# Another written-out order for a fused recurrent-attention and maxout kernel: the first weight group ahead of the inputs, and seventeen waits of GpSimd for VectorE

## The chip, the cores and the metric

One Trainium2 chip; the kernel runs on 1 core of it. The metric is device time in microseconds (us): the median of repeated runs of one program. TensorE (PE, with its weight loads PEld) multiplies, VectorE (DVE), ScalarE (ACT) and GpSimd (POOL) do the elementwise work, and SyncE (SP) issues all the transfers here.

## The reference

Two stages follow each other. The first is a gated linear recurrence over 768 steps for 4 batches of 8 heads of width 48; the second is a feed-forward with a maximum of three products, over 3072 tokens of width 384.

```python
state = alpha[:, :, t, :, None] * state + np.einsum('bhd,bhe->bhde', k[:, :, t], v[:, :, t])
y[:, :, t] = np.einsum('bhd,bhde->bhe', q[:, :, t], state)
...
h = np.maximum(np.maximum(x @ w1, x @ w2), x @ w3)
return (h @ w_out).astype(np.float32)
```

## The kernel before, in words

**Tiles and steps.** A step s of 12 covers 256 tokens of one batch (batch s % 4, chunk s // 4). Inputs of a step sit in rings of four buffers, so step s+4 reuses what step s read. Inside a step the recurrence is done in chunks: decays become factors, keys and queries are multiplied by them, scores are masked, and a state of 48 x 48 per head is carried from chunk to chunk. Everything that TensorE writes goes to one of eight banks, which the order names.

**The maxout.** The three products are not computed apart. The weights are staged in three column groups; `differ` forms w2 - w1 and w3 - w1 of a group (wdif), so the hidden value is w1's product plus the larger of zero and the two differences. w1's part is folded into the output: w1 is copied to half precision, turned on TensorE (`turn_weight`), and multiplied with w_out once (`multiply_weights`).

**What sets the order.** The schedule is manual: each engine executes its instructions in the order in which the program issues them, and that order is the string ORDER (line 580), which `emit` walks. A piece reads `letter, number, engine @ step # banks`. Its engine is v (VectorE), p (GpSimd), a (ScalarE); the pieces without one run on TensorE, or on SyncE if they are transfers. The letters, with the line of the operation in the profile where the prediction speaks of it:

- transfers by SyncE: l0 to l3 load alpha, k, q, v of a step (L81); K0 to K11 load weights (L97, L100), three for each column group (w1, w2, w3), then w_out; D turns a half of a step's q and k by a transposing DMA (L310); W stores (L520)
- gates of the recurrence: m pair product of alpha (L225), N logs (L229), r logs and their exponential (L234, L236), c running sums on TensorE (L251, L254), e and f the factors for k and q (L260), g totals (L270), M gates between chunks (L397)
- keys, queries, values: u and w multiply k and q by the nearer alpha (L239, L242), k and q scale them (L280), V scales v (L188 on ScalarE, L190 on VectorE), v copies values for each chunk (L182, L184)
- T turns q and k on TensorE in steps 0 to 4 (L303), and t copies them out (L182, L184); S state products (L408), s adds the kept state (L420), z decays it (L424), y spreads it
- A scores (L324), a masks them (L335, L339), Y attention into x (L350), x copies x out (L182, L184)
- weights: b copy to half precision, B turn (L449), n keep, d differences (L438), C w_out in half precision, P product (L460)
- G gates of the maxout (L472), h the two maxima (L481, L483, L485), O projections (L506), o scaled output (L188, L190)
- I spreads the mask over rows, Z clears padding, H issues warming matmuls on a blank tile (L525), `H..^name` the same after one small matmul that waits for a named tile (L544).

A group's first three weights are staged in ring buffers of steps 2 and 3 (`staged`): K0 in alpha's third buffer, K1 in q's, K2 in k's. So a load for step 2 waits until the copy and the differences of that group have read them.

A piece with `>name` gets an explicit wait of its first instruction for the named piece's last one; everything else waits only for the data and buffers that it uses.

The lists start in this order of loads: alpha0, alpha1, k0, q0, k1, K1, v0, K0, K2, q1, v1, alpha4. In the list before, twelve pieces carry a `>`.

Of the kernel before, what the change touches and what calls it, by code (L numbers as in the profile page):

```python
# [24 lines left out]
def kernel(  # L25
# [552 lines left out]
    held = mybir.DependencyInfo(mybir.DependencyClass.Sync, mybir.DependencyReason.DATA)  # L578

    ORDER = """  # L580
        l0@0 l0@1 l1@0 l2@0 Z2a@0 m0v@0 l1@1 N0a@0 r0a@0 H10@0#0 c0@0#0 K1@0 e0a@0 m0p@1 I0a@0 l3@0 u0v@0 N0a@1
        K0@0 k0v@0 r1a@0 H7@0#1 c0@1#1 K2@0 f0a@0 w0v@0 e0a@1 l2@1 r0a@1 q0v@0 l3@1 r1a@1 g0a@1 u0v@1 g0a@0
        H6@0#2 T1@0#2 l0@4 T0@0#3 k0p@1>u0@1 t1v@0 t0v@0 V0a@0 H1@0#4 H1^t1@0#4 A1@0#4,5 M0p@1 M0p@0 S0@0#6,7
        d0v@0 s0a@0 f0a@1 z0v@0 b0a@0 a2v@0 K3@0 y0a@0 d1v@0 H2@0#0 H2^d0@0#0 B0@0#0 A0@0#2,3 w0v@1 Y3@0#6 l0@2
        K4@0 q0v@1 K5@0 V0a@1 a1v@0 l2@2 H4@0#1 T0@1#1 a0v@0 T1@1#4 v1p@1>q0@1 t0a@1 a3v@0 S0@1#3,2 l1@2 Z3v@0
        t1a@1 Y0@0#5 s0v@1 m0v@4 r0a@4 v0v@1 K6@0 A0@1#1,4 r1a@4 n0v@0 x0a@0 z0v@1 H1@0#3 A1@1#3,0 a0v@1 x1a@0
        m0p@2>z0@1 y0a@1 a1v@1 H1@0#1 G0@0#1 d2v@0 N0a@2 h0a@0 c0@2#5 b1v@0 r0a@2 K7@0 G2@0#6 d3v@0 N0a@4 K8@0
        r1a@2 a3v@1 e0a@2 l3@2 H1@0#4 G3@0#4 w0p@2>d3@0 h2a@0 a2v@1 c0@4#1 f0a@2 l0@3 Y3@1#6 s1v@1 Y0@1#0 q0v@2
        Y2@1 x0a@1 G1@0#3 K9@0 g0a@4 x1a@1 h3v@0 u0p@2>q0@2 B1@0#2 e0a@4 G2@1#0 h1v@0 n1a@0 k0v@2 G0@1#6 h2a@1
        G3@1#4 g0a@2 f0a@4 d4v@0 h0a@1 T0@2#2 b2a@0 T1@2#3 K10@0 t0v@2 d5p@0>d4@0 G1@1#0 l1@4 t1a@2 s1v@0 h3v@1  # L590
        G4@1#5 K11@0 V0a@2 h1v@1 A0@2#1,6 A1@2#2,3 M0p@2 M1p@0 a0v@2 l0@5 S0@2#7,4 v0p@2 a2v@2 G5@0#0 s0a@2
        v1a@2 l2@4 a1v@2 G5@1#7 z0p@2 a3v@2 m0p@3 G4@0#1 y0a@2 s1v@2 Y0@2#2 z1p@0 N0a@3 Y2@2#6 x0v@2 Y3@2 B2@0#3
        y1p@0 l1@3 x1a@2 c0@3#4 h4a@0 n2v@0 G2@2#2 g0a@3 h4a@1 G1@2#3 u0p@4 h2a@2 h5v@1 G0@2#6 r0a@3 e0a@3 k0v@4
        G5@2#1 C1a@0 G3@2#5 l2@3 M0v@3 C0v@0 C2a@0 G4@2#7 h5v@0 P1@0#2 l3@4 h4v@2 m0p@5>C0@0 h3v@2 P0@0#0 M0p@4
        p1a@0 l3@3 w0v@4 r0a@5 P2@0#7 N0a@5 q0v@4 p0a@0 r1a@3 c0@5#2 p2v@0 T1@4#5 f0a@3 l0@6 e0a@5 u0v@3 T0@4#0
        h5v@2 O0@0#4 t0a@4 l0@7 k0v@3 h0a@2 w0v@3 O1@0#7 f0a@5 l1@5 h1v@2 V0a@4 q0p@3>w0@3 t1v@4 g0a@5 O0@1#1
        l0@8 V0a@3 o1v@0 o0v@0 v1p@4 r1a@5 r0a@6 W0@0 S0@4#0,6 S0@3#3,5 o0a@1 s0v@4 A0@4#2,7 M1p@1 s0v@3 v1a@3
        W1@0 T0@3#4 z0p@4 l2@5 T1@3#0 z0p@3 s1v@4 l1@6 O0@2#1 a1v@4 m0p@6 t1a@3 l3@6 t0v@3 y0p@4 v0a@4 a0v@4
        A1@3#3,6 A1@4#7,0 s1v@3 m0p@7 A0@3#4,2 a2v@3 r1a@6 O1@1#5 N0a@6 a2v@4 m0p@8 o0a@2 a0v@3 v0a@3 l2@6 u0p@5
        c0@6#3 a3v@3 O1@2#7 a1v@3 N0a@7 z1p@1 l0@9 y0a@3 a3v@4 k0p@5 Y1@4#4 Y3@4#1 l3@5 Y0@3#6 Y3@3#2 Y2@3 x0v@3  # L600
        Y0@4 x1a@3 Y2@4 o1v@1 u0p@6 c0@7#0 e0a@6 G1@3#6 o1v@2 x1a@4 N0a@8 w0v@5 G2@3#2 f0a@7 q0v@5 G4@3#1 f0a@6
        e0a@7 c0@8#5 h2v@3 x0a@4 D0@5 G3@3#7 g0a@6 h4a@3 V0v@6 G5@3#2 r0a@7 h3v@3 v1p@6>V0@6 D1@5 e0a@8 G0@3#4
        h5v@3 f0a@8 G4@4#7 m0v@9 h0a@3 k0v@6 G0@4#3 N0a@9 r0a@8 G3@4#1 l1@7 w0v@6 g0a@7 g0a@8 W0@2 V0a@5 G2@4#2
        h1v@3 q0p@6>w0@6 h4v@4 c0@9#4 h0a@4 G5@4#6 l2@7 h2v@4 g0a@9 G1@4#7 h5v@4 M0p@6 f0a@9 D0@6 M1p@4 O1@3#0
        v1p@5 h1v@4 e0a@9 v0a@5 h3v@4 D1@6 M0p@5 M1v@5 M1v@2 u0v@7 A1@5#5,2 v0a@6 A0@5#3,6 S0@5#7,4 O0@3#1 s0v@5
        r0a@9 a2v@5 z0p@5 y1a@1 W0@1 a0v@5 M1p@3 l3@7 z1p@2 O1@4#7 s1v@5 y0p@5 y1a@2 a1v@5 l1@8 a3v@5 k0p@7
        r1a@7 l3@8 r1a@8 Y3@5#5 o1v@4 Y2@5 Y0@5#3 x1a@5 Y1@5 o0v@3 S0@6#4,6 x0a@5 A1@6#2,7 w0p@7 a3v@6 o1a@3
        G4@5#1 W1@1 M0p@7 a2v@6 G5@5#5 q0p@7 s0v@6 G2@5#3 h4v@5 V0a@7 A0@6#0,7 h5v@5 G0@5#2 z0p@6 h2a@5 D1@7
        a0v@6 z1p@4 v0a@7 G1@5#4 a1v@6 z1p@3 G3@5#1 D0@7 h0v@5 y0a@6 y1p@3 O0@4#5 s1v@6 h1v@5 v1p@7 h3v@5 l2@8
        Y3@6#3 o0a@4 z1v@5 Y2@6 l1@9 M0v@8 Y1@6#0 u0v@8 Y0@6 V0a@8 O1@5#7 k0v@8 W0@3 r1a@9 x0a@6 x1v@6 y1a@5  # L610
        S0@7#2,6 l0@10 S0@8#4 s0v@7 y1a@4 A0@7#5,1 W1@2 A1@7#0,3 z0p@7 a1v@7 G0@6#2 l0@11 y0a@7 w0p@8 s0v@8
        G2@6#1 a3v@7 v1a@8 G5@6#4 a2v@7 q0p@8 h2v@6 G4@6#3 h0a@6 a0v@7 G3@6#0 h4a@6 Y3@7#1 z0p@8 h5v@6 D0@8 Y2@7
        Y1@7#2 M0p@9 Y0@7 u0p@9 h3v@6 G1@6#5 r0a@10 x1v@7 l2@9 O0@5#3 m0p@10 s1v@7 D1@8 x0v@7 h1v@6 G0@7#4 o1v@5
        m0v@11 G4@7#0 l1@10 h0a@7 k0v@9 G5@7#1 N0a@11 c0@11#6 l3@9 G2@7#2 e0a@11 N0a@10 G3@7#4 h2v@7 g0a@11
        f0a@11 l3@10 G1@7#5 M1p@7 h4v@7 w0p@9 v0a@8 c0@10#7 h3v@7 O1@6#2 g0a@10 h5v@7 q0p@9 y0a@8 h1v@7 e0a@10
        A0@8#0,4 r1a@10 A1@8#6,1 a0v@8 O0@7#5 M1p@6 D0@9 z1p@6 a2v@8 V0a@9 M0p@10 a1v@8 u0p@10 D1@9 O0@6#0 a3v@8
        V0a@10 o0v@5 f0a@10 k0v@10 Y2@8#6 W0@4 y1a@6 Y0@8#4 W1@4 Y3@8 Y1@8 z1v@7 S0@9#7 x1v@8 x0a@8 S0@10#1
        v0a@10 s0v@9 O1@7#3 l2@10 z0v@9 W1@3 s0v@10 l3@11 z0p@10 l1@11 o1a@6 v0p@9>z0@9 A0@9#4,6 A1@9#7,1 r0a@11
        a1v@9 G0@8#2 y0a@9 a3v@9 v1p@9 G1@8#6 h0a@8 a0v@9 l2@11 G4@8#1 a2v@9 G3@8#4 o0a@6 w0v@10 Y2@9#2 Y1@9#7
        o0a@7 h1v@8 Y0@9 q0p@10>w0@10 Y3@9 G2@8#0 x1a@9 x0a@9 G5@8#6 h4a@8 h2v@8 G0@9#5 r1a@11 D0@10 h5v@8  # L620
        V0a@11 u0p@11 G2@9#2 h3v@8 h0a@9 G5@9#0 D1@10 w0v@11 v0a@11 G1@9#7 k0v@11 G3@9#1 h2a@9 W0@5 q0v@11
        G4@9#6 M0v@11 O0@8#4 h1v@9 D1@11 h4a@9 h3v@9 y0a@10 h5v@9 D0@11 v1a@11 S0@11#5 A0@10#2,6 A1@10#7,1
        O1@9#0 a3v@10 o1a@7 W1@5 W1@6 a0v@10 s0v@11 O1@8#1 W1@7 a2v@10 z0p@11 W0@7 a1v@10 W0@6 v1p@10 A0@11#2,3
        A1@11#5,7 y0p@11 a1v@11 O0@9#6 a0v@11 y1p@7 a2v@11 Y1@10#3 a3v@11 Y0@10 Y2@10#2 x0a@10 Y3@10 Y1@11#5
        Y0@11 x1a@10 Y2@11#7 x0v@11 Y3@11 G1@10#3 x1a@11 o1v@8 o1a@9 G4@10#5 W1@9 G3@11#2 W1@8 h4a@10 G2@10#7
        o0a@9 G2@11#0 G5@10#5 h2v@11 G0@10#6 h3v@11 G0@11#1 h0a@10 h2v@10 G3@10#0 h5v@10 G5@11#2 h3v@10 G4@11#7
        h1v@10 G1@11#6 h0v@11 h4a@11 O0@10#5 h1v@11 h5v@11 O2@11#0 o0a@10 o0a@8 O1@10#7 W0@8 W0@9 W0@10 O3@11
        O4@11#3,5 o0a@11 o1v@10 W1@10 W0@11 O6@11 O5@11 o2a@11 o1v@11 W2@11 W1@11
# [42 lines left out]
```

## Time and profile before

| | |
|---|---|
| runs | 140.74 us median of 3 (139.72 to 141.44) |
| profiled execution | 140.59 us, of which the span is 138.9 |
| granted TensorE clock | 0.996 |
| DMA | 32.32 MB, mean 233 GB/s |

The profile numbers times from the start of the span. A row of the timeline gives start, duration, engine, line, operation, output and inputs with shapes, a count where neighbours are merged, and in brackets how long the engine was idle before it and what ended that. A row of the chain gives start, duration and what it was. Matmuls are pipelined, so the duration of a merged row has a tail that overlaps with the next. A row by stage gives the stage's bounds and length, then busy time of each engine with its count of instructions, the granted clock, the DMA share and GB/s. A row of waits gives who waited for what, in total, how often, and the longest.

### The profile page before, as it was taken

The page shows a single profiled execution, that of the slowest core. Times are in us where ns is not written, and L with a number is a line of the kernel's source. Part 1 is how long each engine was busy: PE and PEld are TensorE (multiplying, and loading weights), DVE is VectorE, ACT ScalarE, POOL GpSimd, SP SyncE. Part 2 cuts the span into 40 slices and gives each one's busy share as a digit, 9 for nine tenths or more (in the row PEclk, how much of TensorE's full clock was granted, in tenths as well). Part 3 has the DMA queues.
Part 4 walks back from the last instruction along what each step waited for, and adds up shares of the span by engine and source line. Part 5 has one row for each costly group of instructions (what it writes and reads, how often), then busy time and mean ns, then how long its engine had stood idle before and what let it go on. Part 6 is the DMA issues. An engine that isn't in the chain of part 4 may idle for free.

```text
span 138.9 us, 5317 instructions
## 1 busy us (share of the span) xinstructions
PE 129.5 (93%) x2231; PEld 94.9 (68%) x2231; DVE 112.2 (81%) x211; ACT 100.1 (72%) x217; POOL 63.2 (45%) x103
## 2 busy tenths in 40 slices
...
GB/s 102 325 341 351 336 326 276 315 288 295 327 238 242 237 322 292 298 186 91 285 155 330 204 293 327 124 187 310 127 246 330 186 168 275 110 111 7 0 170 170
DMA packets 72743, 32.32 MB, mean 233 GB/s; under 512 B 65296, under 2 KB 72720, under 8 KB 72720
## 3 DMA queue, kind: packets, MB, share of 16 engines
...
## 4 chain that ended last, share of the span: by engine, by line
PE 64%; ACT 11%; DVE 10%; issue 4%; POOL 4%; DMA 3%; SPq 1%; POOLq 0%; DVEq 0%; ACTq 0%
PE bank L472 25%; PE bank L506 23%; PE bank L350 6%; DMA qkT<-qk 3%; PE bank L324 3%; PE bank L460 2%; DVE wdif L438 2%; PE bank L408 2%; POOL qk L280 2%; DVE lat L335 2%; PE bank L303 1%; DVE qk L280 1%; POOL gm L397 1%; PE bank L251 1%; DVE rq L242 1%
## 5 line engine op out<-in xcount | busy, mean ns | idle before, releaser
L472 PE MATMUL bank<-xT,wdif 128*128 128x256 f16 x432 | 50.5, 273 | 0.3 <-DVE wdif L438 0.3
L472 PEld LDWEIGHTS <-wdif 128*128 128x128 f16 x432 | 40.9, 98 | 6.7 <-DVE wdif L438 0.7
L339 DVE TENSOR_TENSOR lat<-bank,pmask 128x512 f16<-128x512 f32 x44 | 27.9, 683 | 3.5 <-PE bank L324 3.4
L506 PE MATMUL bank<-wo,hT 128*128 128x384 f16 (+1 forms) x150 | 27.5, 320 | 0.0
L481 DVE TENSOR_TENSOR hT<-bank,h 128x512 f16<-128x512 f32 x36 | 23.5, 684 | 1.2 <-ACT h L485 0.9
L506 PEld LDWEIGHTS <-hT 128*128 128x128 f16 x150 | 14.5, 98 | 8.9
L485 ACT ACTIVATE h<-bank 128x512 f16<-128x512 f32 x23 | 13.7, 604 | 9.4 <-PE bank L472 3.6
L506 PE MATMUL bank<-w1o,xT 128*128 128x384 f16 (+1 forms) x75 | 15.9, 320 | 0.0
L280 POOL TENSOR_TENSOR qk<-rq,ac 128x768 f16<-128x768 f32 x6 | 10.9, 1813 | 9.5 <-ACT ac L260 5.7
L182 ACT CAST xT<-bank 128x384 f16<-128x384 f32 x17 | 7.8, 479 | 8.4 <-PE bank L350 8.2
L188 ACT ACTIVATE ob<-bank,c 128x384 f32<-128x384 f32 (+1 forms) x14 | 7.8, 569 | 7.7 <-PE bank L506 5.8
L483 DVE TENSOR_SCALAR h<-bank 128x512 f16<-128x512 f32 x13 | 8.7, 685 | 5.5 <-PE bank L472 2.8
L525 PE MATMUL bank<-hT 128*128 128x512 f16 x36 | 11.3, 437 | 1.7 <-DVE hT L633 1.3
L182 ACT COPY vu<-vt 64x384 f16<-64x384 f16 x24 | 12.2, 508 | 0.3
L184 POOL COPY vu<-vt 64x384 f16<-64x384 f16 x18 | 9.1, 504 | 7.3 <-DVE qk L280 3.6
L188 ACT ACTIVATE vt<-rv,c 128x768 f16<-128x768 f32 x11 | 10.3, 940 | 2.3 <-DMA rv<-in_v_dram 2.3
L424 POOL TENSOR_TENSOR kept<-fa,gm 128x192 f32<-128x192 f32 x9 | 4.5, 507 | 15.6 <-DVE fa L420 15.5
L225 POOL TENSOR_TENSOR ra<-ra 128x384 f32<-128x384 f32 x8 | 7.9, 998 | 6.7 <-DVE kept L424 2.9
L182 ACT CAST spread<-kept 64x192 f16<-64x192 f32 x28 | 9.7, 347 | 1.1 <-POOL kept L424 0.7
L324 PE MATMUL bank<-qkT 48*64 48x128 f16 x384 | 8.7, 219 | 1.0 <-DMA qkT<-qk 0.5
L190 DVE TENSOR_SCALAR ob<-bank,c 128x384 f32<-128x384 f32 (+1 forms) x11 | 6.3, 593 | 3.9 <-DMA out_dram<-ob 3.2
L324 PEld LDWEIGHTS <-qkT 48*64 48x64 f16 x384 | 6.3, 106 | 3.9 <-issue 2.8
...
## 6 DMA issues: line engine op xcount, KB each, us to landing
...
```

Source lines behind the costliest of these rows:

```text
L182: nc.scalar.copy(out=dst, in_=src)
L184: engines[eng].tensor_copy(out=dst, in_=src)
L188: nc.scalar.mul(dst, src, col)
L280: engines[eng].tensor_mul(dst, src, by)
L324: nc.tensor.matmul(aps[i][to * J:(to + 1) * J, a * U + n, :], qkT[rows, r, 1, p, cols], qkT[rows, :, 0, p, cols], start=True, stop=True)
L339: nc.vector.tensor_mul(lats[s % 2][u][:, i], bank(("aps", s, u, i), [HP, P]), pmask.rearrange("p r j -> p (r j)").unsqueeze(1).broadcast_t ...
L472: nc.tensor.matmul(gps[:, j, :], wdif[:, f, g, jj * P:(jj + 1) * P], xT[:, f].rearrange("p u t -> p (u t)"), start=(f == 0), stop=(f == NF ...
L481: nc.vector.tensor_max(hTs[s % NH][:, 2 * jg:2 * jg + 2, :], gps, h)
L483: nc.vector.tensor_scalar_max(h, gps, 0.0)
L485: nc.scalar.activation(out=h, in_=gps, func=AFT.Relu)
L506: nc.tensor.matmul(ops, lhs, (w1o if what == "x" else wo16)[:, j, cols], start=((what, j) == every[0]), stop=((what, j) == every[-1]))
L525: nc.tensor.matmul(wps, blank[:, :P], blank, start=True, stop=True)
```

## The change

Only the string ORDER differs: 762 pieces before and after, the same computation, another sequence, other banks, and another engine for some of the pieces that can run on several. The launch and all functions are the same.

The first lines of both, which the prediction follows:

```diff
-        l0@0 l0@1 l1@0 l2@0 Z2a@0 m0v@0 l1@1 N0a@0 r0a@0 H10@0#0 c0@0#0 K1@0 e0a@0 m0p@1 I0a@0 l3@0 u0v@0 N0a@1
-        K0@0 k0v@0 r1a@0 H7@0#1 c0@1#1 K2@0 f0a@0 w0v@0 e0a@1 l2@1 r0a@1 q0v@0 l3@1 r1a@1 g0a@1 u0v@1 g0a@0
-        H6@0#2 T1@0#2 l0@4 T0@0#3 k0p@1>u0@1 t1v@0 t0v@0 V0a@0 H1@0#4 H1^t1@0#4 A1@0#4,5 M0p@1 M0p@0 S0@0#6,7
-        d0v@0 s0a@0 f0a@1 z0v@0 b0a@0 a2v@0 K3@0 y0a@0 d1v@0 H2@0#0 H2^d0@0#0 B0@0#0 A0@0#2,3 w0v@1 Y3@0#6 l0@2
+        K0@0 l0@0 K1@0 l0@1 l2@0 b0v@0 l1@0 H8@0#0 B0@0#0 n0v@0 m0p@0 Z2v@0 l1@1 d0v@0 N0a@0 r0a@0 H4@0#1 c0@0#1
+        r1a@0 l3@0 m0v@1 r0a@1 f0a@0 g0a@0 K2@0 N0a@1 w0v@0 I0a@0 H7@0#2 c0@1#2 q0v@0 l2@1 u0v@0 e0a@0 l3@1
+        e0a@1 M0v@0 k0v@0 g0a@1 l0@4 r1a@1 u0v@1 H2@0#3 H4^q0@0#3 T0@0#3 T1@0#4 V0v@0 k0v@1 t1a@0 S0@0#5,6 d1v@0
+        s0a@0 t0a@0 z0v@0 l0@2 f0a@1 w0v@1 H1@0#7 H3^t1@0#7 A0@0#7,0 K3@0 y0a@0 A1@0#1,4 a1v@0 q0p@1>w0@1 K4@0
+        a3v@0 H1@0#5 Y3@0#5 V0a@1 K5@0 a0v@0 l1@2 v0a@1 s1v@0 m0p@4 a2v@0 H1@0#3 H1^a3@0#3 T0@1#3 S0@1#2,0 l2@2
+        t0v@1 M0p@1 T1@1#4 s0v@1 Y0@0#7 t1v@1 K6@0 z0p@1 x0a@0 x1v@0 A1@1#6,1 y0p@1 v1a@1 a3v@1 G0@0#3 m0p@2
+        a2v@1 A0@1#2,4 r0a@2 s1v@1 G1@0#7 N0a@2 d2v@0 b1a@0 c0@2#5 K7@0 d3v@0 e0a@2 K8@0 N0a@4 a0v@1 l3@2 H3@0#1
+        G3@0#1 r1a@2 u0p@2>d3@0 f0a@2 a1v@1 l0@3 c0@4#6 Y3@1#0 f0a@4 Y2@1 k0v@2 Y0@1#2 h0a@0 G2@0#4 g0a@2 x0a@1
+        K10@0 x1v@1 M0p@2 B1@0#3 r0a@4 w0v@2 G2@1#5 e0a@4 n1v@0 G3@1#2 b2a@0 q0v@2 G0@1#0 h2a@0 h1v@0 d4p@0>q0@2
+        h2a@1 T1@2#3 h3v@0 g0a@4 T0@2#4 h0a@1 K11@0 G1@1#7 t1a@2 t0v@2 l2@4 d5p@0 K9@0 h1v@1 G4@1#5 V0a@2 h3v@1
...
-        h1v@10 G1@11#6 h0v@11 h4a@11 O0@10#5 h1v@11 h5v@11 O2@11#0 o0a@10 o0a@8 O1@10#7 W0@8 W0@9 W0@10 O3@11
-        O4@11#3,5 o0a@11 o1v@10 W1@10 W0@11 O6@11 O5@11 o2a@11 o1v@11 W2@11 W1@11
+        G0@11#0 h3v@10 G2@11#1 h5v@11 h0a@11 G3@11#5 h1v@10 h2a@11 G1@11#4 h3v@11 O1@10#3 h1v@11 O2@11#6 o1v@10
+        W1@10 O0@10#7 W0@9 W1@8 O3@11 o0v@10 O4@11#2,0 W0@10 o0v@11 O6@11 O5@11 o2a@11 o1v@11 W2@11 W1@11
```

The loads now start K0, alpha0, K1, alpha1, q0, k0, k1, v0, K2, q1, v1, alpha4. The pieces with an explicit wait are now seventeen:

```
q0p@1>w0@1 u0p@2>d3@0 d4p@0>q0@2 y1p@0>z1@0 w0p@4>z1@0 v0p@3>V0@3 k0p@3>u0@3 u0p@5>M1@1 q0p@5>m0@9
v1p@5>V0@5 y0p@5>z0@5 u0p@7>z0@5 q0p@7>w0@7 q0p@9>w0@9 v0p@10>y1@7 y0p@11>z0@11 v0p@11>z0@11
```

Before, the twelve were:

```
k0p@1>u0@1 v1p@1>q0@1 m0p@2>z0@1 w0p@2>d3@0 u0p@2>q0@2 d5p@0>d4@0 m0p@5>C0@0 q0p@3>w0@3
v1p@6>V0@6 q0p@6>w0@6 v0p@9>z0@9 q0p@10>w0@10
```

Over the whole list, GpSimd gets long scalings (k, q) in 12 places instead of 9 and two differences instead of one; ScalarE copies values (v) in 16 places instead of 12; VectorE copies x in 11 places instead of 7 and scales k or q in 12 places instead of 15. Warming matmuls (L525) go from 36 to 35.

96 lines of the change are left out of this document (48 added, 48 removed).

## The prediction

> **What bounds the kernel now.** I read the page's head and its busy times first, then busy time by stage, then TensorE's waits, then the timeline of the opening.
>
> ```profile
> span 138.9 us, 5317 instructions
> PE 129.5 (93%) x2231; PEld 94.9 (68%) x2231; DVE 112.2 (81%) x211; ACT 100.1 (72%) x217; POOL 63.2 (45%) x103
> ...
> 0.00:24.45 24.45, 19.39 (x307) 10.57 (x307) 19.65 (x47) 19.89 (x45) 8.89 (x21) 1.00 1.02 294
> ...
> 34.73:60.00 25.27, 25.27 (x460) 18.72 (x460) 21.57 (x39) 22.15 (x47) 15.19 (x22) 1.00 1.02 280
> 60.00:90.00 30.00, 29.36 (x566) 22.43 (x565) 27.63 (x54) 22.54 (x52) 19.73 (x31) 1.00 1.07 220
> 90.00:118.00 28.00, 28.00 (x467) 20.86 (x469) 22.85 (x40) 20.03 (x43) 11.55 (x17) 1.00 1.04 228
> 118.00:138.90 20.90, 17.34 (x258) 13.59 (x246) 10.31 (x17) 6.15 (x12) 1.38 (x4) 0.98 0.26 95
> ...
> sum 138.90, PE 11.30 PEld 3.48; mean PE 0.81 PEld 0.25
> ...
> PE bank L324 <- DMA qkT<-qk: 0.5, 1, 0.5
> ```
>
> A stage's row gives its length, then busy time of PE, PEld, DVE, ACT and POOL, the clock, the DMA share and GB/s. The row "sum 138.90" counts the warming matmuls (L525) alone. From 34.73 to 118 TensorE idles 0.64 us, of which 0.5 is one wait for a transposing DMA. So from 34.73 on time is TensorE work, and both orders contain the same. Real TensorE work is 129.5 - 11.3 = 118.2 us; of the other 20.7 us, 24.45 - 19.39 + 11.3 = 16.4 lie before 24.45 and 20.90 - 17.34 = 3.6 in the last stage. Only in the opening can the change gain much; afterwards it can gain about 0.6 and can lose more.
>
> In the opening two things limit: the one queue of loads, and from 12.6 us VectorE.
>
> ```profile
> 5.49 1.00 POOL L225 TENSOR_TENSOR ra<-ra 128x384 f32<-128x384 f32 x1 [1.54 <-DMA ra<-in_alpha_dram]
> 6.64 0.56 DVE L239 TENSOR_TENSOR rk<-rk,ra 128x384 f32<-128x384 f32 x1 [1.83 <-DMA rk<-in_k_dram]
> 12.61 0.96 DVE L438 TENSOR_TENSOR wdif<-rq,ra 128x768 f16<-128x768 f32 x1 [0.35 <-DMA ra<-in_moe_w_dram]
> 16.05 0.94 ACT L188 ACTIVATE vt<-rv,c 128x768 f16<-128x768 f32 x1 [0.93 <-DMA rv<-in_v_dram]
> ...
> 4.25:12.61 8.36, 5.35 (x8) 1.00 1.14 343
> 12.61:24.35 11.74, 11.51 (x22) 1.00 1.09 314
> ...
> 21.90 0.82 PE L472 MATMUL bank<-xT,wdif 128*128 128x256 f16 x6
> 24.49 0.83 PE L472 MATMUL bank<-xT,wdif 128*128 128x256 f16 x6 [0.29 <-DVE wdif L438]
> 29.20 1.06 PE L303 MATMUL bank<-ident,qk 128*128 128x128 f16 x16
> 30.09 1.47 PE L472 MATMUL bank<-xT,wdif 128*128 128x256 f16 x12
> 31.50 0.64 PE L324 MATMUL bank<-qkT 48*64 48x128 f16 x32
> 34.73 0.63 PE L350 MATMUL bank<-lat,vu 128*32 128x128 f16 x32
> ```
>
> The first four rows end at a landing: the second, third, eighth and eleventh load. (16.05 - 5.49)/9 = 1.17 us lies between two landings. The two rows after them are VectorE alone: 3.0 us idle before 12.61, then 0.2 idle in 11.7. The last six are my milestones: first gate G0@0 at 21.90, G3@0 at 24.49, the turns T0/T1@2 at 29.20, G1@1 at 30.09, scores A0@2 at 31.50, attention Y0@2 at 34.73. The first weight group is no limit of G0@0: its difference d0v starts at 12.61 and takes 0.96, so the weights are ready 8.3 us before G0@0.
>
> **The change, part by part.** Loads. The first twelve are the same twelve in both lists, so what follows them keeps its place; only the places inside change. With 1.17 per place (first landing 4.3, an estimate from 5.49 - 1.17) the new landings are: K0 4.3, alpha0 5.5, K1 6.6, alpha1 7.8, q0 9.0, k0 10.2, k1 11.3, v0 12.5, K2 13.7, q1 14.9, v1 16.05. Alpha0 comes 1.2 later, k0 3.5 later.
>
> VectorE gets b0v, n0v, Z2v and d0v early, into the 3.0 us in which it was idle, and gives away both t@0, v0v@1, q0v@1 to ScalarE and GpSimd; it takes V0v@0, k0v@1 and the x1 copies. Prices are these rows (start to start inside a run of ops is a little less than the duration: the three masks below take 1.88, 0.63 each; two hT maxima 1.28):
>
> ```profile
> 16.06 0.96 DVE L280 TENSOR_TENSOR qk<-rq,ac 128x768 f16<-128x768 f32 x1
> 16.94 1.88 DVE L335 TENSOR_TENSOR lat<-bank,rowmask 128x512 f16<-128x512 f32 x3
> 26.80 1.28 DVE L481 TENSOR_TENSOR hT<-bank,h 128x512 f16<-128x512 f32 x2
> 23.48 0.95 DVE L438 TENSOR_TENSOR wdif<-rq,rv 128x768 f16<-128x768 f32 x1
> 15.41 0.55 DVE L242 TENSOR_TENSOR rq<-rq,ic 128x384 f32<-128x384 f32 x1
> 10.98 1.29 DVE L184 COPY qkT<-bank 128x1024 f16<-128x1024 f16 x2 [0.32 <-PE bank L303]
> 17.81 1.93 ACT L182 COPY qkT<-bank 128x1024 f16<-128x1024 f16 x2 [0.83 <-PE bank L303]
> 6.36 1.21 ACT L182 COPY rowmask<-pmask 64x128 f16<-64x128 f16 x4
> L280 POOL TENSOR_TENSOR qk<-rq,ac x6: 1809/1814/1818, 46.3 to 106.4; 128x768 f16<-128x768 f32 x6
> ```
>
> I follow the new list by hand. Step 0: alpha0 5.5, its pair product on GpSimd (1.0) 6.5, ScalarE's logs, sums and exponentials then end with q's factor at 9.0; near_q 9.0 to 9.5, q0v to 10.4, near_k to 10.9. k's factor e0a@0 stands behind the four rowmask copies (1.21), done 11.1; k0v@0 11.1 to 12.0. V0v@0 waits for v0: 12.6 to 13.2; k0v@1 to 14.1; d1v to 15.0. The turned tiles are copied by ScalarE now (0.97 each against 0.65), with s0a between them, done 15.5; scores at 15.6, masks from 16.0. Four masks, s1v, two copies t@1, s0v and x1v (2.4 + 0.3 + 1.2 + 0.3 + 0.5, with 0.1 of waiting) end at 20.8: G0@0 at 20.9, 1.0 ahead of 21.90. Two masks, s1v and d2v, d3v (1.2 + 0.3 + 1.75) end at 24.05: G3@0 at 24.1, 0.4 ahead of 24.49. Now the lead goes: u0p@2 waits for d3v and takes 1.0 on GpSimd, so k0v@2 starts at 25.2; x0a@1 stands on ScalarE behind e0a@2, N0a@4, r1a@2, f0a@2, f0a@4, h0a@0 and g0a@2 and is ready at 27.4. G2@1, G3@1, G0@1 (2.07 for three gates of six matmuls, the row with x18 below) end at 29.5, T1/T0@2 at 30.6: G1@1 at 30.6, 0.5 behind 30.09. d4p moves to GpSimd, waits for q0v@2 (28.5), takes 1.8, ends 30.3; G4@1 needs it only at 31.3, so this costs nothing; if q0v@2 is over a microsecond later it costs all of that. t1a@2 stands behind h0a@1: A0@2 at 32.2. With both scores 0.6, S0@2 0.44 and three gates 2.07, Y0@2 starts at 35.3. TensorE's pieces ahead of Y0@2 are the same set in both lists, so 35.3 - 34.73 = +0.6 is the opening's term. Its ends: -3.0, if all of VectorE's idle time becomes lead; +2.0, one landing (1.17) and one turned copy on ScalarE (0.97) more. I take +0.6, near the middle and what the chain gives.
>
> Warming matmuls go from 36 to 35: no term, they fill waits.
>
> After 35 us engines exchange small pieces. By counts and rows VectorE's total rises 0.4, ScalarE's 0.1 and GpSimd's 0.8 us: nothing. What differs is how far a piece stands ahead of its user. Between the last transposing DMA and the first score of the same step I counted TensorE's work (gate 0.69, projection of nine 1.46, by the two rows below): in steps 5 to 11 it was 6.5, 5.8, 4.9, 6.1, 4.6, 3.9, 3.8 and becomes 4.7, 5.1, 5.5, 4.2, 5.3, 4.5, 3.8.
>
> ```profile
> 67.92 0.89 SPq L310
> ...
> 68.85 4.66 DMA qkT<-qk
> ...
> 76.39 2.07 PE bank L472 x18
> 78.46 1.46 PE bank L506 x9
> ...
> 134.01 0.62 DVE L190 TENSOR_SCALAR ob<-bank,c 128x384 f32<-128x384 f32 x1 [3.19 <-DMA out_dram<-ob]
> 135.38 0.42 DVE L190 TENSOR_SCALAR ob<-bank,c 128x192 f32<-128x192 f32 x1 [0.75 <-PE bank L506]
> ```
>
> Issue and landing took 0.89 + 4.66 = 5.6 us there, and TensorE waited 0.5. Steps 5 and 8 lose 1.8 and 1.9 of distance, but steps 10 and 11 stood at 3.9 and 3.8 without a wait, because the list issues these DMAs ahead of TensorE. Bounds: -0.6 (the idle 0.64 goes) to +3.7. I take +0.5, one more wait like the one shown, as that is the nearest row.
>
> The waits. The entries that name an operation of VectorE to wait for go from 12 to 17; nine of the 17 repeat a data dependence (q0p@1>w0@1, y1p@0>z1@0 and so on). Eight add one: u0p@2, d4p@0, w0p@4, u0p@5, q0p@5, u0p@7, v0p@10, v0p@11. GpSimd is idle 55% of the span, so what queues behind them has room; u0p@2 and d4p are in the chain above.
>
> Tail. The last projection pieces are the same; W1@8 is now issued behind W1@10, and o0v@11 needs its buffer. W1@10 can go 2.1 after the gates' end (129.4), W1@8 lands by 134.5 at the pace of the row at 134.01 (that one too waited for a store), o1v@11 still starts when TensorE ends, 135.4 as now: 0, at most +0.6.
>
> Sum: the profiled execution is 140.59 us, 138.9 of span and 1.7 around it, 0.1% under the median 140.74. 140.59 + 0.6 + 0.5 = 141.7.
>
> **Rivals.** *The early work is a gain.* G0@0 comes 1.0 earlier; if ScalarE's queue does not hold x0a@1, that lead and half of the other 2.0 survive: 140.6 - 2.0 = 138.6; all of it, 137.6. For it: VectorE's 3.0 idle. Against: ScalarE is busy 19.89 of 24.45, and gets the turned copies.
>
> *It doesn't do what it says.* G0@0 never waited for weights, and Y0@2 starts where it did: 140.6.
>
> *Transposes late.* If steps 5, 6 and 8 each wait what they lost (1.8, 0.7, 1.9, less 1.0 of the slack that steps 10 and 11 show): +3.4, beside the opening's 0.6: 140.6 + 0.6 + 3.4 = 144.6. It decides when a transpose needs over 5 us at a distance under 5.
>
> *The two engines in each other's way.* This is the one on the other side of a gain that I hold likeliest:
>
> ```profile
> L397 POOL TENSOR_TENSOR gm<-ge x9: 193/202/909, 12.6 to 97.4; 128x4 f32<-128x4 f32 x9
> ```
>
> One of nine such products took 909 ns instead of 202: it began at 12.6, beside VectorE's wdif that ran from 12.61 to 13.57, and ended with it. GpSimd's long products (1.81) rise from 10 to 14 with the wdif on GpSimd, and those without a wait for VectorE from 5 to 8 (k0p 4, q0p 3, d5p 1). If two of the three more hold a two-input VectorE op for 1.8 in the stage from 60 to 90, where VectorE has 30.00 - 27.63 = 2.4 free, at a place where a mask is awaited: +3.6, 140.6 + 0.6 + 3.6 = 144.8. It decides from two such meetings on. The Trainium skill, GPSIMD Engine Reference, Specifications, says that GpSimd shares its SBUF interfaces with VectorE, with contention when VectorE has two SBUF inputs or a two-port mode; the held product agrees, and no row here shows VectorE held.
>
> **How the numbers follow.** Forecast 0.45 (own range 139.8 to 143.4), unchanged 0.10, gain 0.17, transposes late 0.13, engines in each other's way 0.15. Two per cent, about what a measurement tells from no change, is 137.9 and 143.6. Of the gain 0.10 lies under 137.9; the two slow cases lie above 143.6 but for 0.02, and the forecast adds 0.01: faster 0.10, same 0.63, slower 0.27. The range 138.6 to 145.0 leaves half of the gain (0.08) and about 0.12 of the slow cases outside.
>
> **What would show it.** In the changed profile: first load landings near 4.3 and 5.5; G0@0 near 20.9; G1@1 near 30.6; Y0@2 near 35.3; TensorE idle about 1.1 us from there to 118. G0@0 later than 22 breaks the VectorE chain. G1@1 before 29 means ScalarE's queue is no limit. VectorE two-input ops of over 1.2 us mean the port. Long waits at L324 for qkT mean the transposes. I am wrong if Y0@2 moves by over 2 us, or TensorE idles over 3 us after it.

## The result, and the profile after

| | before | changed |
|---|---|---|
| median of 6 runs each, one chip | 140.76 us (139.72 to 141.44) | 142.73 us (141.56 to 143.2) |
| ratio | | 1.013, 95% [1.0082, 1.0177] |
| the same program once more, another chip | 140.69 us, 35 runs | 142.09 us, 12 runs; 1.005 [1.0005, 1.0095] |
| profiled execution, of which the span | 140.59, 138.9 | 142.71, 141.0 |

The time lies inside the range and 1.0 us above the predicted 141.7: no change by two per cent, with both intervals just above 1. The ratios here and below leave out executions more than 1.5% above the fastest of their program, so that a ratio can differ from the quotient of two medians.

First the head of the changed kernel's page and its busy time by stage, in the columns of the prediction.

```profile
span 141.0 us, 5302 instructions
...
0.00:24.45 24.45, 19.02 (x306) 10.42 (x307) 19.61 (x47) 17.64 (x40) 9.19 (x22) 1.00 0.99 285
24.45:34.73 10.28, 9.13 (x185) 7.35 (x183) 9.93 (x16) 8.92 (x21) 5.54 (x6) 1.00 0.96 285
34.73:60.00 25.27, 25.27 (x460) 18.63 (x458) 23.72 (x47) 22.94 (x51) 11.48 (x16) 1.00 1.01 278
60.00:90.00 30.00, 28.40 (x517) 22.04 (x515) 22.62 (x45) 25.66 (x60) 22.18 (x29) 1.00 1.05 219
90.00:118.00 28.00, 28.00 (x494) 21.53 (x493) 25.34 (x49) 19.05 (x38) 13.39 (x19) 1.00 1.06 221
```

Ahead of 118 us TensorE idles again in two places only. One is the opening, which now reaches past 34.73: 1.15 us of idle time (10.28 - 9.13) fall in the second row. The other is the stage from 60 to 90, with 1.60 us (30.00 - 28.40) where before had 0.64.

Next the timeline: three operations that wait for a load, then the prediction's milestones with S0@2 added (G0@0, G3@0, G1@1, A0@2, S0@2, Y0@2), then the scores of step 6 with their weight load, and the last scaled output.

```profile
7.28 0.96 DVE L438 TENSOR_TENSOR wdif<-rq,ra 128x768 f16<-128x768 f32 x1 [0.65 <-DMA rq<-in_moe_w_dram]
13.81 0.62 DVE L190 TENSOR_SCALAR vt<-rv,c 128x768 f16<-128x768 f32 x1 [0.49 <-DMA rv<-in_v_dram]
32.91 0.94 ACT L188 ACTIVATE vt<-rv,c 128x768 f16<-128x768 f32 x1 [1.09 <-DMA rv<-in_v_dram]
...
21.82 0.83 PE L472 MATMUL bank<-xT,wdif 128*128 128x256 f16 x6 [0.15 <-DVE xT L184]
25.14 0.83 PE L472 MATMUL bank<-xT,wdif 128*128 128x256 f16 x6 [0.21 <-DVE wdif L438]
30.75 0.82 PE L472 MATMUL bank<-xT,wdif 128*128 128x256 f16 x6
32.63 0.64 PE L324 MATMUL bank<-qkT 48*64 48x128 f16 x32
33.90 0.44 PE L408 MATMUL bank<-vt,qk 64*64 64x48 f16 x32 [0.62 <-ACT vt L188]
36.34 0.63 PE L350 MATMUL bank<-lat,vu 128*32 128x128 f16 x32
...
75.75 0.29 PEld L324 LDWEIGHTS <-qkT 48*64 48x64 f16 x16 [1.75 <-DMA qkT<-qk]
75.79 0.42 PE L324 MATMUL bank<-qkT 48*64 48x128 f16 x16 [1.60 <-ACT ic L236]
...
137.47 0.42 DVE L190 TENSOR_SCALAR ob<-bank,c 128x192 f32<-128x192 f32 x1 [0.22 <-PE bank L506]
```

Read the brackets of the first three rows. K1 landed at 7.2 instead of the predicted 6.6, v0 at 13.8 instead of 12.5. The third row is V0a@2, the scaling of v of step 2: it waited 1.09 us for its load, where before it waited for none, and S0@2 then waited 0.62 for it. Y0@2 is at 36.34 instead of 34.73; but A0@2, which does not read v, was already 1.13 late. The scores of step 6 wait for their transposed keys: the bracket of the matmul names ScalarE, that of its weight load the DMA, which landed at 75.7.

Before, the two rows that answer to these read:

```profile
31.25 0.98 ACT L188 ACTIVATE vt<-rv,c 128x768 f16<-128x768 f32 x1
73.56 0.42 PE L324 MATMUL bank<-qkT 48*64 48x128 f16 x16 [0.54 <-DMA qkT<-qk]
```

The whole difference can be laid out on three milestones.

| | before | changed | difference |
|---|---|---|---|
| start to A0@2 | 31.50 | 32.63 | +1.13 |
| A0@2 to Y0@2 | 3.23 | 3.71 | +0.48 |
| Y0@2 to the scores of step 6 | 38.83 | 39.45 | +0.62 |
| from there to the end | 65.34 | 65.21 | -0.13 |
| span | 138.9 | 141.0 | +2.10 |

The tail is as it was: 3.53 us lie from the last output's start to the end of the span, 3.52 before (138.9 - 135.38).

### The profile page after: what moved, and what is told of

The parts are those of the page before. It is cut to its first block, busy times and chain, and to the rows that moved or that the text cites. A ratio compares the mean times of both kernels' runs of the same rounds, so it can differ in the third digit from the quotient of the medians.

```text
span 141.0 us, 5302 instructions
## 1 busy us (share of the span) xinstructions
PE 129.3 (92%) x2231; PEld 94.8 (67%) x2231; DVE 113.2 (80%) x219; ACT 101.3 (72%) x218; POOL 63.5 (45%) x94
## 4 chain that ended last, share of the span: by engine, by line
PE 72%; SPq 11%; DMA 9%; DVE 2%; ACT 2%; issue 1%
PE bank L472 30%; PE bank L506 26%; DMA rv<-in_v_dram 9%; SPq L81 6%; PE bank L350 6%; SPq L97 5%; PE bank L324 4%; PE bank L460 2%; PE bank L408 2%; PE bank L303 1%; PE bank L251 1%; DVE qk L280 1%; ACT vt L188 1%; DVE wdif L438 1%; PE bank L254 0%
## 5 line engine op out<-in xcount | busy, mean ns | idle before, releaser
L280 POOL TENSOR_TENSOR qk<-rq,ac 128x768 f16<-128x768 f32 x7 | 12.7, 1820 | 17.2 <-DVE rq L242 17.1
L188 ACT ACTIVATE ob<-bank,c 128x384 f32<-128x384 f32 (+1 forms) x16 | 9.1, 572 | 11.5 <-PE bank L506 10.2
L182 ACT COPY vu<-vt 64x384 f16<-64x384 f16 x32 | 16.3, 509 | 0.5
L525 PE MATMUL bank<-hT 128*128 128x512 f16 x35 | 11.2, 443 | 1.3 <-DVE hT L633 1.3
L184 POOL COPY vu<-vt 64x384 f16<-64x384 f16 x12 | 6.0, 500 | 13.3 <-DVE vt L190 6.9
L182 ACT CAST xT<-bank 128x384 f16<-128x384 f32 x13 | 6.1, 482 | 6.5 <-PE bank L350 6.1
L280 POOL TENSOR_TENSOR qk<-rk,ic 128x768 f16<-128x768 f32 x5 | 9.1, 1821 | 1.0 <-DVE rk L239 0.8
L188 ACT ACTIVATE vt<-rv,c 128x768 f16<-128x768 f32 x9 | 8.4, 932 | 1.3 <-DMA rv<-in_v_dram 1.1
L506 PEld LDWEIGHTS <-xT 128*128 128x128 f16 x75 | 6.4, 98 | 3.3
L182 ACT CAST spread<-kept 64x192 f16<-64x192 f32 x24 | 8.3, 346 | 0.3
L229 ACT ACTIVATE la<-ra 128x384 f16<-128x384 f32 x12 | 6.2, 521 | 3.2 <-POOL ra L225 2.8
```

The lines of the kernel that those rows point to most:

```text
L182: nc.scalar.copy(out=dst, in_=src)
L188: nc.scalar.mul(dst, src, col)
L280: engines[eng].tensor_mul(dst, src, by)
L506: nc.tensor.matmul(ops, lhs, (w1o if what == "x" else wo16)[:, j, cols], start=((what, j) == every[0]), stop=((what, j) == every[-1]))
L525: nc.tensor.matmul(wps, blank[:, :P], blank, start=True, stop=True)
```

## The experiments

Runs are compared with the kernel before on the same chip.

**Which half of the list costs?** Two crosses: one has the changed list up to Y0@2 and the old one behind it, the other the reverse, with banks renamed at the seam. The lines at the seam:

```diff
-        G5@0#6 y0a@2 m0v@3 Y0@2#0 s1v@2 Y2@2#3 N0a@3 Y3@2 M1v@0 x0v@2 B2@0#4 l3@3 x1a@2 z1v@0 c0@3#7 h4a@1 Z3v@0
+        G5@0#6 y0a@2 m0v@3 Z3v@0 M1p@0 s1v@2 Y0@2#0 z1p@0 N0a@3 Y2@2#3 x0v@2 Y3@2 B2@0#4 y1p@0 l1@3 x1a@2 c0@3#7
```

> The changed kernel's list up to Y0@2, then what is left of the list before, in its own order, with the banks renamed so that they meet. Theory A (the loss is made in the opening, 1.6 us at Y0@2, and the changed rest adds 0.5): 140.8 + 1.6 = 142.4, Y0@2 near 36.3. Theory B (the loss is made after Y0@2 by waits of the changed rest): 141.0 to 141.3.

> The opposite cross: the list before up to Y0@2, then the changed rest. Theory A: 140.8 + 0.5 = 141.3, Y0@2 near 34.7, with the wait of 1.6 us for the step-6 scores still there. Theory B: 142.4 or more.

Before ran at 141.92. The changed opening with the old rest took 145.56 us (1.0258 [1.0196, 1.032]), the old opening with the changed rest 144.53 (1.0156 [1.0083, 1.0229]). Neither theory's number came. The first cross is slower than either whole list, so the halves don't add; the second can't be told from the changed list's 1.005 to 1.013. Two of TensorE's waits in the first cross, whose profiled execution is the longest of its six:

```profile
PE bank L460 <- DVE wo L184: 2.0, 1, 2.0
PE bank L408 <- ACT ac L260: 1.9, 1, 1.9
```

Neither wait is in either whole list. The first ends at 42.89, soon behind the seam: TensorE waits for a copy of w_out that VectorE makes. The second ends at 105.14, far behind it: there ScalarE had stood 2.01 us for a load of v. What the crosses do tell: Y0@2 is at 35.40 with the changed opening and at 35.15 with the old one, and the wait at the step-6 scores goes with the rest (0.3 with the old one, 1.3 with the changed). Their totals contain costs that neither whole list has, and can't price a half.

**The loads' sequence alone.** The old list, with only its first loads put in the changed sequence.

```diff
-        l0@0 l0@1 l1@0 l2@0 Z2a@0 m0v@0 l1@1 N0a@0 r0a@0 H10@0#0 c0@0#0 K1@0 e0a@0 m0p@1 I0a@0 l3@0 u0v@0 N0a@1
-        K0@0 k0v@0 r1a@0 H7@0#1 c0@1#1 K2@0 f0a@0 w0v@0 e0a@1 l2@1 r0a@1 q0v@0 l3@1 r1a@1 g0a@1 u0v@1 g0a@0
+        K0@0 l0@0 K1@0 l0@1 Z2a@0 m0v@0 l2@0 N0a@0 r0a@0 H10@0#0 c0@0#0 l1@0 e0a@0 m0p@1 I0a@0 l1@1 u0v@0 N0a@1
+        l3@0 k0v@0 r1a@0 H7@0#1 c0@1#1 K2@0 f0a@0 w0v@0 e0a@1 l2@1 r0a@1 q0v@0 l3@1 r1a@1 g0a@1 u0v@1 g0a@0
```

> The list before, all as it was, only SyncE's first twelve loads stand in the changed sequence (K0, alpha0, K1, alpha1, q0, k0, k1, v0, K2, q1, v1, alpha4). Theory L (the loads' sequence delays the opening): alpha0 and k0 land 1.2 and over 3 us later, Y0@2 over 1 us late, 141.8 to 142.8. Theory C (the sequence is harmless; what delays is the turned copies on ScalarE and its long queue): 140.6 to 141.2. Theory L says so although nothing but loads moved, so VectorE's early weight work of the changed kernel cannot help here.

It took 144.5 us, 1.0213 [1.0168, 1.0257], with G0@0 at 25.14 and Y0@2 at 37.96, 3.2 later than before. TensorE waits for VectorE's product of q and k:

```profile
PE bank L303 <- DVE qk L280: 2.8, 2, 2.3
```

So loading the first weights first costs some 3 us by itself, more than the 1 to 2 that the theory of the loads' sequence expected; k0 lands 3.7 us later (10.3 against 6.6). The rest of the changed opening pays that back: with the same sequence its G0@0 is at 20.61 to 21.82. That the early work on VectorE does it is argued from the prediction's chain and was not tried by itself.

This run also shows a VectorE product that takes longer beside a GpSimd one:

```profile
14.04 1.81 POOL L280 TENSOR_TENSOR qk<-rk,ic 128x768 f16<-128x768 f32 x1 [5.11 <-DVE rk L239]
15.43 1.24 DVE L438 TENSOR_TENSOR wdif<-rq,ra 128x768 f16<-128x768 f32 x1
```

VectorE's difference began 1.4 us into GpSimd's product and took 1.24 instead of 0.95.

**The seventeen waits.** The changed list without any `>`.

```diff
-        s0a@0 t0a@0 z0v@0 l0@2 f0a@1 w0v@1 H1@0#7 H3^t1@0#7 A0@0#7,0 K3@0 y0a@0 A1@0#1,4 a1v@0 q0p@1>w0@1 K4@0
+        s0a@0 t0a@0 z0v@0 l0@2 f0a@1 w0v@1 H1@0#7 H3^t1@0#7 A0@0#7,0 K3@0 y0a@0 A1@0#1,4 a1v@0 q0p@1 K4@0 a3v@0
...
-        G3@0#1 r1a@2 u0p@2>d3@0 f0a@2 a1v@1 l0@3 c0@4#6 Y3@1#0 f0a@4 Y2@1 k0v@2 Y0@1#2 h0a@0 G2@0#4 g0a@2 x0a@1
+        G3@0#1 r1a@2 u0p@2 f0a@2 a1v@1 l0@3 c0@4#6 Y3@1#0 f0a@4 Y2@1 k0v@2 Y0@1#2 h0a@0 G2@0#4 g0a@2 x0a@1 K10@0
```

> The changed kernel without its seventeen explicit waits of GpSimd for VectorE; the waits for data stay. If the eight waits that are more than data cost time (u0p@2 and d4p@0 in the opening): 141.5 to 142.3. If they protect VectorE from GpSimd's long products: 143.5 to 146, with two-input VectorE products over 1.2 us. If neither: 142.7.

143.2 us against 141.92: 1.0079 [1.0031, 1.0128], between the changed kernel's own 1.005 and 1.013. As a whole the waits neither cost nor save what could be measured. One of them did do something visible. Without its wait d4p starts together with VectorE's product q0v@2:

```profile
15.49 1.64 SPq L97 DMA_DIRECT2D rv<-in_moe_w_dram  x1
28.61 2.64 POOL L438 TENSOR_TENSOR wdif<-rv,rk 128x768 f16<-128x768 f32 x1 [1.24 <-DMA rv<-in_moe_w_dram]
28.62 0.95 DVE L280 TENSOR_TENSOR qk<-rq,ac 128x768 f16<-128x768 f32 x1
```

GpSimd took 2.64 us for what takes it 1.82 with the wait (next experiment), and VectorE its usual 0.95. Counted from the start of VectorE's product, GpSimd's ended after 2.63 us without the wait (28.61 + 2.64 - 28.62) and after 2.85 with it (28.69 + 1.82 - 27.66): of a head start of 1.0 the meeting left 0.2. V of step 2 landed late here too, at 33.0, and Y0@2 is at 36.37.

**The changed kernel once more.** No edit.

> The changed kernel once more, as the yardstick of this call and as a second profile of the same program: 1.013 of the time before. If the landing times of the opening's loads vary between executions (theory L2), the landings of K1 and of v0 differ from the first profile by about 0.5 and 1.2 us and G0@0 lies nearer 20.8 than 21.8, while the wait of 1.6 us for the step-6 scores stays.

142.09 us against 140.69, 1.005 [1.0005, 1.0095]. Its timeline, with the products of VectorE and GpSimd and SyncE's issue that answer to the rows above:

```profile
span 138.7 us, 5302 instructions
...
15.40 0.58 SPq L97 DMA_DIRECT2D rv<-in_moe_w_dram  x1
20.61 0.83 PE L472 MATMUL bank<-xT,wdif 128*128 128x256 f16 x6
24.17 0.83 PE L472 MATMUL bank<-xT,wdif 128*128 128x256 f16 x6 [0.25 <-DVE wdif L438]
27.66 0.95 DVE L280 TENSOR_TENSOR qk<-rq,ac 128x768 f16<-128x768 f32 x1
28.69 1.82 POOL L438 TENSOR_TENSOR wdif<-rv,rk 128x768 f16<-128x768 f32 x1 [2.00 <-DVE qk L280]
29.78 1.61 PE L472 MATMUL bank<-xT,wdif 128*128 128x256 f16 x12
31.20 0.94 ACT L188 ACTIVATE vt<-rv,c 128x768 f16<-128x768 f32 x1 [0.35 <-DMA rv<-in_v_dram]
34.62 0.63 PE L350 MATMUL bank<-lat,vu 128*32 128x128 f16 x32
73.54 0.42 PE L324 MATMUL bank<-qkT 48*64 48x128 f16 x16 [1.07 <-DMA qkT<-qk]
```

The same program, 2.3 us shorter in span: 1.72 of it lies before Y0@2, 0.53 between Y0@2 and the step-6 scores. Here every load down to the eleventh landed within 0.1 us of the predicted place (K0 4.3, K1 6.5, alpha1 7.8, q0 9.0, v0 12.5, K2 13.7, v1 16.1), and Y0@2 is where before has it. The opening's loss in the first profile is therefore no property of the list alone; it is that of loads which landed late in that execution, by 0.6 at K1 and 1.2 to 1.3 from v0 on. This profile is one of the two shortest of the program's twelve executions (140.44 us, against a median of 142.09): it shows no loss to before at all, and the 0.5% of the median has no profile of its own.

**What v of step 2 decides.** Two edits of one exchange each: K3@0 (the fourth weight load) against alpha2, as a change of the load order that should do nothing, and v2 against K8@0, which brings v2 forward by one place.

```diff
-        s0a@0 t0a@0 z0v@0 l0@2 f0a@1 w0v@1 H1@0#7 H3^t1@0#7 A0@0#7,0 K3@0 y0a@0 A1@0#1,4 a1v@0 q0p@1>w0@1 K4@0
+        s0a@0 t0a@0 z0v@0 K3@0 f0a@1 w0v@1 H1@0#7 H3^t1@0#7 A0@0#7,0 l0@2 y0a@0 A1@0#1,4 a1v@0 q0p@1>w0@1 K4@0
```

> The changed kernel with K3@0 and l0@2 exchanged in the list, so that SyncE issues a weight load (free to go) ahead of the load that waits for d1v. Theory S (SyncE held by d1v starves the loads): the loads of K4 to v2 land 0.5 to 1 earlier, Y0@2 0.5 to 1 earlier. Theory L (the loads are limited by their rate, SyncE is ahead of them): landings from the fifteenth load on within 0.3, no difference.

```diff
-        a2v@1 A0@1#2,4 r0a@2 s1v@1 G1@0#7 N0a@2 d2v@0 b1a@0 c0@2#5 K7@0 d3v@0 e0a@2 K8@0 N0a@4 a0v@1 l3@2 H3@0#1
+        a2v@1 A0@1#2,4 r0a@2 s1v@1 G1@0#7 N0a@2 d2v@0 b1a@0 c0@2#5 K7@0 d3v@0 e0a@2 l3@2 N0a@4 a0v@1 K8@0 H3@0#1
```

> The changed kernel with l3@2 and K8@0 exchanged, so that step 2's v is the twenty-first load and not the twenty-second. Theory V (Y0@2 is late because S0@2 waits for V0a@2 and that for v2): S0@2's wait of 0.6 goes, Y0@2 0.6 to 1.0 earlier, 0.4 to 1.0 us faster. Theory C (ScalarE's queue ahead of V0a@2 is as late anyway): no difference, V0a@2 starts at once behind t1a@2 but not earlier than 32.5.

K3 first: 141.81 us, 1.0045 [1.0003, 1.0086]. V2 first: 141.69 us, 1.0032 [0.9994, 1.007]. Against the changed kernel's 1.005 on the same chip neither differs measurably; the theory of v2 had expected 0.4 to 1.0 us. In the profile of the second v2 landed at 29.7, where the changed kernel has 31.2 and 32.8, and V0a@2 no longer waited for a load:

```profile
31.01 1.02 ACT L188 ACTIVATE vt<-rv,c 128x768 f16<-128x768 f32 x1
34.57 0.79 PE L350 MATMUL bank<-lat,vu 128*32 128x128 f16 x32
```

Put the start of V0a@2 beside Y0@2 for all profiles in which V0a@2 waited for its load. The last column says how long v2 held TensorE: the way from A0@2 to Y0@2, less the 2.89 us that it takes in the two profiles with v2 early enough (31.55 to 34.44 with step 6's k on VectorE, 31.68 to 34.57 with v2 first).

| kernel | V0a@2 | Y0@2 | between | A0@2 | held by v2 |
|---|---|---|---|---|---|
| changed, first | 32.91 | 36.34 | 3.43 | 32.63 | 0.82 |
| changed, second | 31.20 | 34.62 | 3.42 | 31.32 | 0.41 |
| without waits | 32.95 | 36.37 | 3.42 | 32.10 | 1.38 |
| changed opening, old rest | 31.97 | 35.40 | 3.43 | 32.10 | 0.41 |
| K3 first | 31.38 | 34.80 | 3.42 | 31.84 | 0.07 |
| transfers behind (below) | 32.15 | 35.58 | 3.43 | 31.56 | 1.13 |
| the same with k on VectorE (below) | 32.82 | 36.24 | 3.42 | 33.16 | 0.19 |

The distance is always scaling (0.94), one state product (0.44) and three gates (2.1), less their overlaps. So in these seven v2's landing is what ends last ahead of Y0@2, but it accounts for 0.07 to 1.38 us only; the rest of a late Y0@2 is there at A0@2 already, through the earlier loads and VectorE's chain. With v2 out of the way Y0@2 was at 34.44 and 34.57, no earlier to speak of than in the second profile (34.62). The kernel before has 0.34 of the same kind (3.23 less 2.89), but there ScalarE came to V0a@2 late and the load was in. The landing itself varied from 30.3 to 33.0 with v2 in its old place.

**Step 6: what holds the transposes?** Two theories. T: GpSimd makes both k and q of step 6 and is late. P: SyncE hands out the transposes late, and slowly, because of the transfers ahead of them in its queue. First k to VectorE:

```diff
-        h2a@4 k0p@6 G5@4#1 N0a@8 D0@5 h1v@3 r1a@8 c0@8#0 h4v@3 y1a@1 c0@9#7 G5@3#2 l3@6 e0a@8 M0p@6 W0@1 G4@4#4
+        h2a@4 k0v@6 G5@4#1 N0a@8 D0@5 h1v@3 r1a@8 c0@8#0 h4v@3 y1a@1 c0@9#7 G5@3#2 l3@6 e0a@8 M0p@6 W0@1 G4@4#4
```

> The changed kernel with one letter changed: k0p@6 becomes k0v@6, the scaling of step 6's keys on VectorE (0.95) instead of GpSimd (1.8). Theory T (the transposes of step 6 start late because GpSimd scales the keys and then the queries one after the other): the transposes start 1.3 to 1.8 earlier, the wait of 1.6 for the scores is under 0.4, 0.9 to 1.4 us faster than the changed kernel. Theory P (the transposes are late because SyncE and the loads hold them): no difference.

143.05 us, 1.0034 [0.9984, 1.0084]: no gain that can be told from the changed kernel's 1.005 on that chip. The profiled execution took 143.05 us, the median. In it the products were done at 64.7, the first transpose started at 66.92 all the same, and TensorE waited 2.0 at the scores. T falls: early products wait in SyncE's queue. Behind this one pause the granted clock fell to 0.50 (mean 0.59 from 74 to 78), and the 36 gate matmuls took 5.41 us instead of 4.10. GpSimd's part of the gain was also eaten:

```profile
74.00:78.00 4.00, 3.46 (x61) 2.70 (x62) 2.48 (x7) 2.66 (x6) 0.00 (x0) 0.59 1.13 322
...
62.07 0.96 DVE L280 TENSOR_TENSOR qk<-rk,ic 128x768 f16<-128x768 f32 x1
62.14 2.56 POOL L280 TENSOR_TENSOR qk<-rq,ac 128x768 f16<-128x768 f32 x1
```

Beside VectorE's product GpSimd's took 2.56 instead of 1.82.

Then the queue itself: the load l3@6, a store (W0@1) and the load l3@7 moved from between the two pairs of transposes to behind the second.

```diff
-        h2a@4 k0p@6 G5@4#1 N0a@8 D0@5 h1v@3 r1a@8 c0@8#0 h4v@3 y1a@1 c0@9#7 G5@3#2 l3@6 e0a@8 M0p@6 W0@1 G4@4#4
-        q0p@6 g0a@9 h5v@3 g0a@8 o1a@2 G3@4#3 l3@7 h4v@4 f0a@8 G1@4#2 h0a@4 h3v@4 M0p@8 r0a@9 D0@6 M1p@4 O1@3#4
-        M0p@5 h5v@4 M1p@3 r1a@9 z1v@4 f0a@9 V0v@5 D1@6 e0a@9 h1v@4 A1@5#3,5 v0a@5 v1p@5>V0@5 A0@5#0,6 S0@5#1,7
+        h2a@4 k0p@6 G5@4#1 N0a@8 D0@5 h1v@3 r1a@8 c0@8#0 h4v@3 y1a@1 c0@9#7 G5@3#2 e0a@8 M0p@6 G4@4#4 q0p@6
+        g0a@9 h5v@3 g0a@8 o1a@2 G3@4#3 h4v@4 f0a@8 G1@4#2 h0a@4 h3v@4 M0p@8 r0a@9 D0@6 M1p@4 O1@3#4 M0p@5 h5v@4
+        M1p@3 r1a@9 z1v@4 f0a@9 V0v@5 D1@6 l3@6 W0@1 l3@7 e0a@9 h1v@4 A1@5#3,5 v0a@5 v1p@5>V0@5 A0@5#0,6
```

> The changed kernel with three transfers of SyncE (the load l3@6 and the two writes W0@1's and l3@7's places) moved behind the second pair of transposes of step 6 (D1@6). Theory P (SyncE hands out the transposes of step 6 late because of what stands ahead of them in its queue): the transposes D@6 start within 0.2 us of the end of GpSimd's q product of step 6, where the two profiles of the changed kernel have 0.1 to 0.6 us, and the wait of TensorE at the step-6 scores falls from 1.1 to 1.6 us to 0.6 to 1.0; time 0 to 0.6 us below the changed kernel. Rival (the transposes take their 7 us from issue to landing whatever stands ahead, and the product's end sets the issue): no difference, wait 1.0 to 1.7, ratio to before 1.003 to 1.010.

147.23 us against 140.69, 1.0444 [1.0383, 1.0505]: far slower than either theory said. The transposes did get faster, as P says. SyncE's rows and the view of the tile qkT, which gives the issue's duration in ns and the time to landing, first of the changed kernel (second profile), where the first transpose of step 6 is shown, then of the edit, where both are:

```profile
63.77 0.85 SPq L81 DMA_DIRECT2D rv<-in_v_dram  x1
64.72 0.52 SPq L520 DMA_DIRECT2D out_dram<-ob  x1
65.28 0.43 SPq L81 DMA_DIRECT2D rv<-in_v_dram  x1
65.88 4.29 SPq L310 DMA_TRANSPOSE qkT<-qk  x2
...
L310 SPq DMA_TRANSPOSE qkT<-qk x1: 2937/2937/2937, 65.9 to 65.9; - x1
DMA to landing us min/median/max: 6.7/6.7/6.7
```

```profile
62.00 7.37 SPq L310 DMA_TRANSPOSE qkT<-qk  x4
...
L310 SPq DMA_TRANSPOSE qkT<-qk x2: 1233/1242/1252, 66.8 to 68.1; - x2
DMA to landing us min/median/max: 2.7/2.7/2.7
```

With two loads of 384 KB and a store just ahead, the transpose held SyncE for 2.94 us and landed 6.7 us after its issue; with none, 1.23 and 2.7. The list before has a load, a store and a load there too, the first of them issued 1.0 us earlier, and 5.0 us to landing. But the scores need both transposes, and from the first issue to the second landing it is 7.3 us before (66.20 to 73.5), 7.5 in the changed kernel's second profile (65.88 to 73.4) and 4.0 in the edit (66.79 to 70.8): the transposes are slow in both whole lists alike. Nor are they issued very late in the changed one, 0.08 and 0.62 us behind the end of GpSimd's product in its two profiles. In the edit the turned q and k of step 6 were there at about 70.8 (68.1 + 2.7), some 6 us ahead of the scores that read them. What cost the time was the load moved back:

```profile
75.02 0.93 ACT L188 ACTIVATE vt<-rv,c 128x768 f16<-128x768 f32 x1 [5.27 <-DMA rv<-in_v_dram]
77.21 0.42 PE L324 MATMUL bank<-qkT 48*64 48x128 f16 x16 [3.79 <-ACT ob L188]
79.14 6.88 PE L472 MATMUL bank<-xT,wdif 128*128 128x256 f16 x36 [1.26 <-ACT xT L182]
...
80.00:82.00 2.00, 2.00 (x11) 1.45 (x10) 0.65 (x2) 1.94 (x5) 1.23 (x1) 0.50 1.18 326
```

L3@6 is v of step 6. ScalarE's V0a@6 stood 5.27 us waiting for it; behind it in the list stands o0a@3, which has to empty the bank that the scores write. And TensorE's pause brought a second cost: the granted clock (the third number from the end) fell to 0.50, and the 36 gate matmuls took 6.88 us, where the changed kernel's second profile has 4.10 for them. Scores 3.67 later than in that profile (0.96 of it from the opening), gates 5.0, the next scores 7.8, and the span is 7.8 longer (146.5 against 138.7).

The same, with k of step 6 on VectorE, and with v2 one place earlier besides:

```diff
-        h2a@4 k0p@6 G5@4#1 N0a@8 D0@5 h1v@3 r1a@8 c0@8#0 h4v@3 y1a@1 c0@9#7 G5@3#2 e0a@8 M0p@6 G4@4#4 q0p@6
+        h2a@4 k0v@6 G5@4#1 N0a@8 D0@5 h1v@3 r1a@8 c0@8#0 h4v@3 y1a@1 c0@9#7 G5@3#2 e0a@8 M0p@6 G4@4#4 q0p@6
```

> The same, and the k product of step 6 taken from GpSimd to VectorE (alone, that edit had its products ready some 2 us earlier, and SyncE's queue held the transposes). Theory P: with both, the transposes of step 6 start some 1.0 to 2.0 us earlier than in the changed kernel (65.9 by its second profile), the wait at the step-6 scores falls to 0.4 or below, and the time is 0.7 to 1.4 us below the changed kernel: ratio to before 0.995 to 1.000. Rival (what is late at the scores of step 6 is made up or given back later: another wait takes the place, at VectorE's evictions or at the gate): wait gone, time as the changed kernel, ratio 1.003 to 1.010.

> The same as the last, and the load of v of step 2 (l3@2) changed places with the load of the ninth weight block (K8@0), which alone brought that load in at 29.7 instead of 31.2 to 33.0 us. Theory P with the opening's late landings as the second cause: Y0@2 begins at 34.6 or before, no wait for vt ahead of S0@2, wait at the step-6 scores 0.4 or below; ratio to before 0.990 to 0.998. Rival (the two causes aren't the whole of the loss, the rest lies in many small places of the middle stages): ratio 1.000 to 1.006 in spite of both waits gone.

145.59 us (1.0323 [1.0262, 1.0385]) and 144.97 us (1.0168 [1.0091, 1.0244]). In the first the transposes of step 6 started 30.1 us behind Y0@2 instead of 31.3, 1.2 us less, as P expected, but P's time (0.995 to 1.000 of before) did not come. V of step 6 was again the last to come: TensorE waited 1.3 at the scores for the bank that ScalarE empties, and 2.1 at the gate behind them, and the granted clock was 0.89 from 75 to 90. In the second v2 landed at 30.0 and V0a@2 did not wait, as in the exchange alone; Y0@2 was at 35.20 all the same, as TensorE waited 0.6 for one of GpSimd's differences: with v2 out of the way the next piece is close. Neither beats the kernel before; a list that keeps l3@6 where it is and moves only the store and l3@7 was not tried.

**The kernel before once more.** No edit.

> The kernel before, unchanged: a control for the comparison and a second profile of its loads. All theories: ratio 1.000 within 0.004; Y0@2 begins at 34.5 to 35.2, wait at the step-6 scores 0.3 to 0.6. Theory L (the landing times of the queued loads vary from execution to execution, whatever the list): loads 1 to 11 within 0.3 us of the first profile or late by 0.5 or more from some load on, as in the changed kernel. Rival (only the changed list's sequence is disturbed): all within 0.3.

140.98 against 140.69 us, 0.9996 [0.9961, 1.0032].

```profile
span 139.3 us, 5317 instructions
...
34.90 0.63 PE L350 MATMUL bank<-lat,vu 128*32 128x128 f16 x32
73.61 0.42 PE L324 MATMUL bank<-qkT 48*64 48x128 f16 x16 [0.50 <-DMA qkT<-qk]
```

Its first eleven loads landed within 0.1 us of the first profile's, v2 at 30.5 (first profile 30.9; old opening with the changed rest 31.4). The old opening's three profiles have Y0@2 at 34.73, 34.90 and 35.15. The eight profiles with the changed opening and v2 in its place, six of them with some other edit, run from 34.44 to 36.37, 35.47 in the mean: 0.5 more. That the changed sequence makes its loads land late more often is likely from these numbers (v0 late by over 1 us in two of the ten profiles with the changed opening, in none of the old one's three), but so few don't show it.

## Why the prediction was right, and where its steps were off

**The opening's term, +0.6.** The size holds in the mean (+0.5 over the profiles) but the step that carried it failed, so the agreement is in part luck. The prediction let the lead be lost on ScalarE's queue (x0a@1, then t1a@2) and ended the chain at A0@2. When the loads came in time, the lead of 1.3 at G0@0 shrank to 0.3 at G3@0, nearly as forecast, and ScalarE's queue took little more: x0a@1 was ready at 26.8 instead of 27.4, G1@1 at 29.78 and A0@2 at 31.32 where 30.6 and 32.2 were forecast. What ends last ahead of Y0@2 is v2's landing through V0a@2 and S0@2, which the prediction did not name; it said of all loads behind the twelfth that they keep their place. The place they kept; the time of landing they did not. In the first profile late landings gave +1.61, 1.13 of it at A0@2 by way of the early loads and the rest by v2; in the second it was -0.11.

**Landings.** First at 4.3, spacing 1.17: right within 0.1 for eleven loads in one execution of the changed kernel, up to 1.3 too early in the other (v0 13.8). The spread is the term that the prediction had no bound for.

**G0@0 at 20.9, G3@0 at 24.1.** 20.61 and 24.17 in the second profile, 21.82 and 25.14 in the first: the hand-followed chain on VectorE is right given its landings.

**The middle's term, +0.5.** One more wait at the transposes of one step, and it is step 6. TensorE's idle time from 60 to 90 rose by 0.96 in the first profile (1.60 against 0.64), and the way from Y0@2 to the step-6 scores by 0.62 and 0.09. So the size fits the first profile and is too large for the second, where what the wait takes is nearly all made up elsewhere. The distance in TensorE's work, by which steps 5 and 8 should have been the worst, is not what decides. Nor does the changed list bring the transposes later: the second landed 38.8 us behind Y0@2 before (73.5 - 34.73) and in the second profile (73.4 - 34.62), 39.4 in the first. The prediction priced issue and landing at 5.6 us; the pair took 7.3 from its first issue.

**Rivals.** *Transposes late* (+3.4) did not come: steps 5 and 8 had no such wait. *Engines in each other's way*: the waits, or the order, kept them apart in the changed kernel. VectorE's 768-wide products took 0.95 to 0.96 us throughout, GpSimd's 1.80 to 1.83, and its small products 195 to 220 ns, without the 909 of before. Where an edit let them meet, GpSimd paid when the two began together, VectorE when it began in the middle of a GpSimd product (1.24 with the loads alone, 1.19 with v2 first). *A gain* did not come either; the earliest Y0@2 seen, 34.44, is 0.3 ahead of before, not 2.

**The waits, tail and warming at nothing:** the waits made no difference that the intervals of 1.0079 and of 1.005 to 1.013 would tell; the tail measured 3.53 against 3.52; the warming was not tried by itself. "Wrong if Y0@2 moves by over 2 us" was nearly met by one profile: 1.61.
